# Unread identity products in TensorE's opening waits, and other owners for two PSUM tiles of the last group

## The chip, the cores and the metric

The kernel is one program on one core of a Trainium2 chip. A core has five engines that run side by side, each through its own queue of instructions in order: TensorE (PE, matrix products into PSUM; PEld is its weight load), VectorE (DVE), ScalarE (ACT), GpSimd (POOL) and SyncE (SP, which here only issues DMAs). SBUF is the working memory of 128 partitions. PSUM is the memory that TensorE writes and VectorE and ScalarE read. The metric is device time of one execution in microseconds (us).

## The reference

Two stages follow each other. The first is a delta-rule recurrence for 4 batches of 8 heads, 768 steps, 48 dimensions, in fp32:

```
k_n = k / (norm(k) + 1e-6)
for t in range(768):
    y[t]  = q[t] @ state
    state = state + beta[t] * outer(k_n[t], v[t] - k_n[t] @ state)
```

The second takes the 3072 x 384 result as x and computes a feed-forward layer of three branches with a maximum:

```
h   = max(max(x @ w1, x @ w2), x @ w3)      # 384 -> 768
out = h @ w_out                              # 768 -> 384
```

## The kernel before, in words

**Tiling.** The 768 steps are cut in 12 chunks of 64. Inside a chunk the recurrence becomes a triangular system whose inverse `ut` is made on VectorE (the generator `solve`, L507, one column per step) and applied by small matrix products. Four blocks of 32 steps and 4 batches by 8 heads fill the 128 partitions of one solve. Two chunks (512 tokens) are a group; there are six. The feed-forward layer of a group (`ffn`, L1213) runs between the pieces of the next group's recurrence.

**Order.** Everything stands under a manual schedule: each engine runs its instructions in the order in which the program emits them. The opening is a straight list of calls, from L1298 on, followed by `ffn(0)`. In it `turn` (L322) transposes keys or queries of a unit by TensorE into the PSUM tile `p_t`, which ScalarE or VectorE copies out (L344). `gram` (L404) makes the products of keys with keys, and of keys with queries, in `p_g` (L415), copied out by ScalarE at L426 and L432. `some(solving, HB + 1)` lets VectorE run the solver of the first group (L561 and L565, then a transpose at L573), and copies to `ut` follow on VectorE and ScalarE (`placed`, L505). After that come, for chunk 0, `halves_z` (`p_e`, L685), `halves_u` (`p_f`, L696), `join_z` (`p_z`, L713), `join_u` (`p_j`, L726), `new` (`p_u`, L771), `to_y` (`p_y`, L813) and `to_x` (`p_x`, L832). Each needs a copy out of PSUM of the one before it (L688, L700, L717, L728, L776, L817, L839). Between them VectorE and ScalarE unpack weights (`weights`, L230, with its work at L247 to L263), and VectorE makes transposes (L630, L632, L645, L647) and masks (L399). Then `ffn(0)` begins with `p_h` (L1224), and chunk 1 and the solver of the second group run between its products.

**A helper that exists before.** `busy(n, of)` (L1290) takes a tile `p_w` from the PSUM pool `ps_ffn` (two buffers, shared with `p_h`, `p_o` and `p_e` of L1163) and multiplies the identity by `of` n times into it; nobody reads the tile. It is called once, `busy(6, ident)`, ahead of the first transposes.

**The last group.** Its first layer is done by `crossed_hidden` (L1125) in six units of eight products, four products and a `yield`, then four more. The function `bank(n)` hands out the PSUM tile of product n: 0 to 5 from a pool of six buffers (`p_c`), 6 and 7 from the two buffers of `ps_ffn` (`p_e`). Products 0, 2, 3 and 4 are copied out by ScalarE (L1184, L1190, L1193, L1197). Products 1, 5, 6 and 7 are added by VectorE (`result`, L1169 and L1171), which in the units of odd number also adds four sums (L1198 to L1201) ahead of 5, 6 and 7. The second layer (`outputs`, L969) then takes the same two `ps_ffn` buffers as `p` and `q` for its products (L985).

Of the kernel before, what the change touches and what calls it, by code (L numbers as in the profile page):

```python
# [23 lines left out]
def kernel(  # L24
# [31 lines left out]
    nc = tc.nc  # L56
# [10 lines left out]
    TOK = 512  # L67
# [21 lines left out]
    def ps_ffn(shape, name):  # L89
        return psum.tile(shape, FP32, name=name, tag="ffn", bufs=2)  # L90
# [10 lines left out]
    ident = const.tile([128, 128], FP32, name="ident")  # L101
# [34 lines left out]
    def place(n):  # L136
        return n % NK if n < 12 else n % 4
# [82 lines left out]
    def fetch(queue=nc.scalar):  # L220
        if fetched[0] < len(pieces):
            _, src, (a, b) = pieces[fetched[0]]
            st = work.tile([128, 2 * 384], U32, name="w_bits", bufs=5)
            queue.dma_start(
                out=st.rearrange("p (a b) -> p a b", a=a), in_=src
            )
            staged.append(st)
            fetched[0] += 1
# [93 lines left out]
    def turn(n, parts=(0, 1), copy=nc.scalar.copy):  # L322

        if n not in kqts:
            if n == 6:
                kqts[n] = work.tile([128, KT, TOK], FP32, name="xt").rearrange(
                    "p k t -> p (k t)"
                )[:, 0 : NP * 4 * C].rearrange(
                    "p (j b i t) -> p j b i t", b=2, i=2, t=C
                )  # L330
            else:
                kqts[n] = work.tile([128, NP, 2, 2, C], FP32, name="kqt", bufs=6)
        kqt = kqts[n]
        p_t = ps_two("p_t")
        for i in parts:
            src = (kpad[place(n)], qpad[n % NQ])[i]
            for j in range(NP):
                nc.tensor.transpose(
                    p_t[:, i, j * 128 : (j + 1) * 128],
                    src[:, 2 * j : 2 * j + 2],  # L340
                    ident,
                )
        some = slice(parts[0], parts[-1] + 1)
        copy(  # L344
            kqt.rearrange("p j b i t -> p i (j b) t")[:, some],
            p_t.rearrange("p i (x t) -> p i x t", t=C)[:, some],
        )
# [291 lines left out]
    def halves_t(c, parts=(0, 1)):  # L639
        if c not in fine:  # L640
            fine[c] = [square("t") for g in range(2)]
        src = [ut[c % NU][:, g].rearrange("p h x -> p (h x)") for g in range(2)]
        dst = [t.rearrange("p h x -> p (h x)") for t in fine[c]]
        if 0 in parts:
            nc.vector.transpose(out=dst[0], in_=src[0])  # L645
        for bb in range(2) if 1 in parts else ():
            nc.vector.transpose(out=dst[1][rows(1 - bb)], in_=src[1][rows(bb)])  # L647
# [25 lines left out]
    def span(hs):  # L673
        return slice(hs[0], hs[-1] + 1)

    def halves_z(c):
        if c > 1:
            halves_t(c)
        at = [ats[2 * c + g] for g in range(2)]
        second = ut[c % NU].rearrange("p g h (f two x) -> p g h f two x", two=2, x=HB)  # L680
        for hs, p_v, copy in heads_of(c, "p_e", BL):
            for i, h in enumerate(hs):
                for bb, g in TILES:
                    r = rows(bb)
                    nc.tensor.matmul(  # L685
                        p_v[rows(bb ^ g), g, i], at[g][r, h], second[r, g, h, :, 1]
                    )
            copy(zs[c % NU][:, :, span(hs)], p_v)  # L688
# [436 lines left out]
    def crossed_hidden(m, hs):  # L1125

        banks = upper_pool("banks")
        xt, vec = xts[m], nc.vector.tensor_tensor  # L1130
        plus = vec if m == GROUPS - 1 else nc.gpsimd.tensor_tensor
        lo, hi = slice(0, 256), slice(256, 512)
        a11, a12, a13 = (xt[:, t, lo] for t in range(KT))
        a21, a22, a23 = (xt[:, t, hi] for t in range(KT))
        spare = [t.rearrange("p a h d -> p (a h d)") for t in kmore]
        s1, s2, s3, s4 = (spare[0][:, 256 * n : 256 * (n + 1)] for n in range(4))
        parts = [
            work.tile([128, 2, HB * BL + HB], FP32, name=name, bufs=1).rearrange(
                "p s r -> p (s r)"
            )  # L1140
            for name in ("x_bl", "y_bl")
        ]
        vec(out=s3, in0=a11, in1=a21, op=ALU.subtract)
        vec(out=s1, in0=a21, in1=a22, op=ALU.add)
        vec(out=s2, in0=s1, in1=a11, op=ALU.subtract)
        vec(out=s4, in0=a12, in1=s2, op=ALU.subtract)
        x_sums[m] = s1, s2, s3, s4
        for j in range(FT):
            hs[j] = square("h").rearrange("p h c -> p (h c)")
        for unit in range(2 * PAIRS):  # L1150
            j, i = divmod(unit, 2)
            w = {
                name: t[:, 128 * j : 128 * (j + 1)]
                for name, t in thirds[1 + i].items()
            }
            top, bottom = hs[j], hs[j + PAIRS]
            held = parts[unit % 2]
            m1, m5, m6, m7 = (held[:, 256 * n : 256 * (n + 1)] for n in range(4))
            c11 = spare[1][:, 256 * (unit // 2 % 2) :][:, 0:256]

            def times(to, *terms):
                for n, (stays, moves) in enumerate(terms):
                    nc.tensor.matmul(  # L1163
                        to, w[stays], moves, start=(n == 0), stop=(n == len(terms) - 1)
                    )

            def result(h, base, p, spare=None):
                to = h if i == 0 else base if spare is None else spare
                vec(out=to, in0=base, in1=p, op=ALU.add)  # L1169
                if i:  # L1170
                    nc.vector.scalar_tensor_tensor(  # L1171
                        out=h, in0=h, scalar=0.0, in1=to, op0=ALU.max, op1=ALU.max
                    )

            def bank(n):
                if n > 5:
                    return ps_ffn([128, TOK], "p_e")[:, 0:256]
                return banks.tile([128, TOK], FP32, name="p_c", tag="one", bufs=6)[
                    :, 0:256
                ]  # L1180

            p = bank(0)
            times(p, ("b11", a11))
            nc.scalar.copy(m1, p)  # L1184
            p = bank(1)
            times(p, ("b21", a12), ("c1", a13))
            result(top[:, lo], m1, p, c11)
            p = bank(2)
            times(p, ("t3", s3))
            nc.scalar.copy(m7, p)  # L1190
            p = bank(3)
            times(p, ("t1", s1))
            nc.scalar.copy(m5, p)  # L1193
            yield
            p = bank(4)
            times(p, ("t2", s2))
            nc.scalar.copy(m6, p)  # L1197
            plus(out=m6, in0=m6, in1=m1, op=ALU.add)  # L1198
            plus(out=m1, in0=m6, in1=m5, op=ALU.add)
            plus(out=m7, in0=m7, in1=m6, op=ALU.add)  # L1200
            plus(out=m5, in0=m5, in1=m7, op=ALU.add)  # L1201
            p = bank(5)
            times(p, ("c2", a13), ("b22", s4))
            result(bottom[:, lo], m1, p)
            p = bank(6)
            times(p, ("t4", a22), ("c1", a23))
            result(top[:, hi], m7, p)
            p = bank(7)
            times(p, ("c2", a23))
            result(bottom[:, hi], m5, p)  # L1210
            yield
# [64 lines left out]
    def some(gen, n):  # L1276
        for _ in range(n):
            if next(gen, gen) is gen:
                break
# [7 lines left out]
    nc.vector.memset(warm, 1.0)  # L1287
    nc.scalar.sqrt(warm, warm)

    def busy(n, of):  # L1290
        p_w = ps_ffn([128, TOK], "p_w")[:, 0 : of.shape[1]]
        for _ in range(n):
            nc.tensor.matmul(p_w, ident, of)

    def keys(n, queues=one_queue, copy=nc.scalar.copy):
        gram(n, (0,), queues, copy)

# [30 lines left out]
    keys(4)  # L1328
    keys(5)
    turn(6, (0,))  # L1330
    turn(0, (1,))
    load_q(3, (nc.gpsimd, nc.gpsimd))
    load_beta()
    keys(6)
    gram(0, (1,), None, later=True)
    turn(7, (0,))
    turn(1, (1,))
    keys(7)
    turn(2, (1,))
    gram(1, (1,), None, later=True)  # L1340
    turn(3, (1,))
    some(conv, 1)
    gram(2, (1,), None, later=True)
    gram(3, (1,), None, later=True)
    some(solving, HB + 1)
    halves_t(0)
    halves_z(0)
    first_norms()
# [4 lines left out]
    blocks(1, nc.gpsimd)  # L1353
    for _ in range(2):
        fetch(nc.gpsimd)
    halves_u(0)
    turn_t1(0)
    join_z(0)
    masked(pts[0], by_par(pts[0]))
# [2 lines left out]
    masked(pts[1], by_par(pts[1]))  # L1362
    old_k(0)
    old_q(0)
    new(0)
    some(conv, 1)
    fetch(nc.gpsimd)
    load_v(1, nc.gpsimd)
    placed(1, 3)
    to_y(0)  # L1370
    halves_t(1)
    solving = solve(1)
    some(solving, 1)
    to_x(0)
    some(conv, 1)


# [177 lines left out]
```

## Time and profile before

| What | Value |
|---|---|
| Median of three runs | 509.49 us (506.69, 509.49, 509.79) |
| Profiled execution, its own time | 507.8 us |
| Its span, first to last instruction | 506.1 us |
| PE busy | 484.4 us, 96% of the span |
| DVE busy | 362.5 us, 72% |
| ACT / POOL busy | 168.7 us / 186.4 us |
| Mean granted clock of TensorE | 0.969 of full speed |
| Time idle on PE from 0 to 63.3 us | 14.3 us of 63.3 us |

The span is drawn in 40 slices of 12.65 us. In the row of an engine a digit is its busy share in tenths; in the row PEclk it is the clock that TensorE was granted, in tenths of full speed. Lines with a letter L name the line of the program that issued an instruction. "Idle before" gives how long the engine stood still ahead of an instruction and what ended that. A busy TensorE is not one at full speed, so its busy share and its clock are read side by side.

### The profile page before, as it was taken

How to read it: one execution, taken by the hardware profiler on the slowest of the kernel's cores; microseconds unless marked ns; L12 is line 12 of the kernel's file. 1: busy time of each engine (PE TensorE's matmuls, PEld its weight loads, DVE VectorE, ACT ScalarE, POOL GpSimd, SP SyncE). 2: the span in 40 equal slices, each digit the busy share in tenths (PEclk: the TensorE clock that was granted, in tenths of full speed). 3: DMA queues.
4: the chain of work that ended last, by engine and by line, in shares of the span. 5: the costliest groups of instructions: out<-in, count | busy, mean ns of one | idle time of the engine just before them, and what ended most of it. 6: DMA issues, size and time to landing. Idle time of an engine off the chain costs nothing.

```text
span 506.1 us, 18677 instructions
## 1 busy us (share of the span) xinstructions
PE 484.4 (96%) x8064; PEld 338.0 (67%) x8064; DVE 362.5 (72%) x835; ACT 168.7 (33%) x320; POOL 186.4 (37%) x311
## 2 busy tenths in 40 slices
PE   7678899999999999999999999999999999999996
PEld 6567688756565555565555565555797457998795
DVE  5888989868996431799562999565998865467843
ACT  4576854884422142210153200252211042113210
POOL 6424582783491925870495870601000020000000
PEclk9855999999999999999999999999999999999999
DMA  8937979783055925443585552834224321330002
GB/s 111 205 53 207 201 177 147 183 220 91 2 141 128 191 57 122 121 118 99 120 157 124 138 139 62 168 56 93 63 61 88 62 66 25 89 80 0 0 17 47
DMA packets 109122, 53.50 MB, mean 106 GB/s; under 512 B 92209, under 2 KB 102865, under 8 KB 109041
## 3 DMA queue, kind: packets, MB, share of 16 engines
q1 hardware_dynamic: 97280, 31.78, 31.2%
q0 software_dynamic: 9216, 19.85, 15.6%
q8 instruction: 63, 1.03, 0.9%
q10 hardware_dynamic: 2544, 0.69, 0.7%
q14 instruction: 19, 0.15, 0.1%
HBM read 39.17 MB, written 13.11 MB: 103 GB/s over the span
## 4 chain that ended last, share of the span: by engine, by line
PE 82%; DVE 6%; DMA 5%; ACT 2%; issue 1%; SPq 1%; POOL 1%; ACTq 0%; DVEq 0%; POOLq 0%
PE p_h L1224 31%; PE p_o L985 13%; PE p_o L1262 12%; PE p_c L1163 4%; PE p_g L415 3%; PE p_u L771 3%; PE p_m L905 2%; PE p_k L743 2%; PE p_y L813 2%; PE p_q L743 2%; PE p_s L794 2%; PE p_j L726 2%; DMA x_bl<-at_d 1%; DMA qall<-in_q_dram 1%; PE p_e L1163 1%
## 5 line engine op out<-in xcount | busy, mean ns | idle before, releaser
L1224 PE MATMUL p_h<-xt,w_sb 128*128 128x512 f32 (+1 forms) x450 | 187.5, 559 | 1.3 <-issue 0.7
L1224 PEld LDWEIGHTS p_h<-xt,w_sb 128*128 128x128 f32 x450 | 82.5, 193 | 70.0 <-issue 62.4
L1238 DVE TENSOR_TENSOR h<-h,p_h 128x512 f32<-128x512 f32 (+1 forms) x42 | 25.4, 606 | 47.2 <-PE p_h L1224 45.7
L565 DVE TENSOR_TENSOR y_bl<-y_bl,tmp 128x31 f32<-128x31 f32 (+20 forms) x139 | 50.3, 362 | 4.8
L561 DVE TENSOR_TENSOR tmp<-x_bl,y_bl 128x31 f32<-128x31 f32 (+20 forms) x139 | 48.7, 350 | 3.9
L1262 PE MATMUL p_o<-wo_sb,h 128*128 128x384 f32 x144 | 48.9, 490 | 0.0
L373 POOL DMA_DIRECT2D turned<-in_q_dram x72 | 39.1, 551 | 4.3 <-POOL turned L368 2.9
L1262 PEld LDWEIGHTS p_o<-wo_sb,h 128*128 128x128 f32 x144 | 26.8, 190 | 17.2
L1234 ACT ACTIVATE h<-p_h 128x512 f32<-128x512 f32 x24 | 14.3, 597 | 69.3 <-PE p_h L1224 69.2
L263 POOL TENSOR_TENSOR w_sb<-mant,up 128x384 int32<-128x384 int32 x18 | 18.8, 1046 | 37.7 <-DVE mant L259 34.7
L415 PEld LDWEIGHTS p_g<-kqt 48*64 48x64 f32 x1216 | 24.9, 143 | 9.3 <-issue 6.7
L415 PE MATMUL p_g<-kqt 48*64 48x64 f32 (+1 forms) x1216 | 28.1, 243 | 0.9 <-ACT kqt L344 0.8
L1268 ACT COPY o_sb<-p_o 128x384 f32<-128x384 f32 x12 | 5.7, 479 | 62.6 <-PE p_o L1262 56.5
L399 DVE TENSOR_TENSOR pt<-p_g,mask 128x512 f32<-128x512 f32 x20 | 13.8, 689 | 16.2 <-PE p_g L415 16.0
L801 DVE TENSOR_TENSOR st<-st,p_s 48x768 f32<-48x768 f32 (+1 forms) x18 | 17.1, 949 | 11.1 <-PE p_s L794 10.8
L598 POOL DMA_DIRECT2D ut<-y_d x4 | 2.6, 651 | 60.4 <-DMA y_d<-y_bl 60.4
L148 POOL DMA_DIRECT2D v_t<-in_v_dram x14 | 11.5, 829 | 36.0 <-PE p_u L771 36.0
L368 POOL MEMSET turned<- 128x96 f32 x18 | 3.3, 191 | 49.6 <-DVE kqt L389 49.6
L771 PEld LDWEIGHTS p_u<-v_t,ut 64*64 64x64 f32 x768 | 13.7, 144 | 7.9 <-issue 5.9
L432 ACT COPY at<-p_g 128x512 f32<-128x512 f32 x22 | 12.7, 583 | 18.6 <-DVE pt L399 16.1
L373 POOL DMA_DIRECT2D turned<-in_k_dram x32 | 17.4, 553 | 1.2 <-POOL turned L368 1.2
L129 POOL DMA_DIRECT2D kpad<-in_k_dram x24 | 16.4, 691 | 3.0 <-PE p_s L794 3.0
(241 smaller groups left out, 909.2 us busy)
## 6 DMA issues: line engine op xcount, KB each, us to landing
w_bits<-in_moe_w_dram SPq DMA_DIRECT2D x9, 384.0 KB, 5.8
w_bits<-in_moe_w_dram POOLq DMA_DIRECT2D x9, 384.0 KB, 6.3
turned<-in_q_dram POOLq DMA_DIRECT2D x72, 48.0 KB, 2.8
out_dram<-o_sb SPq DMA_DIRECT2D x36, 96.0 KB, 2.3
y_x<-y SPq DMA_DIRECT2D x32, 96.0 KB, 2.2
qall<-y_x SPq DMA_DIRECT2D x32, 96.0 KB, 2.6
v_t<-in_v_dram POOLq DMA_DIRECT2D x14, 192.0 KB, 5.0
at_d<-at SPq DMA_DIRECT2D x72, 32.0 KB, 2.5
```

The costliest lines, as they stand in the source:

```text
L263: nc.gpsimd.tensor_tensor(out=dst.bitcast(I32), in0=mant_v.bitcast(I32), in1=up_v, op=ALU.add)
L373: (queue, nc.gpsimd)[i].dma_start(out=t[p0 : p0 + 32, bb, at : at + NP * 2 * D].rearrange("p (j x) -> p j x", j=NP), in_=(k, q)[i][2 * bb ...
L415: nc.tensor.matmul(p_g[rows(bb ^ (g * i)), par, c0 : c0 + C * (1 + whole)], kq[:, 0], kq if whole else kq[:, i],)
L561: nc.vector.tensor_tensor(out=t_v, in0=row.to_broadcast(t_v.shape), in1=column.to_broadcast(t_v.shape), op=ALU.mult,)
L565: nc.vector.tensor_tensor(out=rest, in0=rest, in1=t_v, op=ALU.subtract)
L743: nc.tensor.matmul(p_b[rows(bb), par, c0 : c0 + D], kqt[g][dims(par), j, bb ^ g, i], st[dims(par), bb ^ g, g, j],)
L771: nc.tensor.matmul(p_v[rows(bb ^ g), g, i], ut[c % NU][rows(bb), g, h], rhs[rows(bb), g, h],)
L985: nc.tensor.matmul(to[:, g], a[j][:, 128 * g : 128 * (g + 1)], b[j], start=(start and g == j == 0), stop=(stop and g == 1 and j == len(a) ...
L1163: nc.tensor.matmul(to, w[stays], moves, start=(n == 0), stop=(n == len(terms) - 1))
L1224: nc.tensor.matmul(p_h, w_sb[i][:, t, f * 128 : (f + 1) * 128], xt[:, t, lo : lo + w], start=(t == 0), stop=(t == KT - 1),)
L1238: nc.vector.tensor_tensor(out=h, in0=h, in1=p_h, op=ALU.max)
L1262: nc.tensor.matmul(p_o, stays, moves, start=(n == 0), stop=(n == len(terms) - 1))
```

## The change

`busy` moves up in the file, and its second argument is the identity unless one is given. Ten calls of it are put into the opening, 76 products of 128 x 128 x 128 in fp32, each of which TensorE runs as two matmul instructions with a weight load each. And in `crossed_hidden` the two buffers of `ps_ffn` go to products 3 and 4 of a unit, while 6 and 7 take theirs from the pool of six.

```
+    def busy(n, of=None):
+        of = ident if of is None else of
+        p_w = ps_ffn([128, TOK], "p_w")[:, 0 : of.shape[1]]
+        for _ in range(n):
+            nc.tensor.matmul(p_w, ident, of)
...
             def bank(n):
-                if n > 5:
+                if n in (3, 4):
                     return ps_ffn([128, TOK], "p_e")[:, 0:256]
...
     turn(6, (0,))
+    busy(5)
     turn(0, (1,))
...
     turn(7, (0,))
+    busy(13)
     turn(1, (1,))
     keys(7)
     turn(2, (1,))
     gram(1, (1,), None, later=True)
+    busy(14)
     turn(3, (1,))
     some(conv, 1)
     gram(2, (1,), None, later=True)
     gram(3, (1,), None, later=True)
     some(solving, HB + 1)
+    busy(24)
     halves_t(0)
     halves_z(0)
...
+    busy(4)
     halves_u(0)
+    busy(2)
     turn_t1(0)
     join_z(0)
...
     old_q(0)
+    busy(3)
     new(0)
+    busy(2)
...
     to_y(0)
+    busy(5)
     halves_t(1)
     solving = solve(1)
     some(solving, 1)
     to_x(0)
+    busy(4)
     some(conv, 1)
```

## The prediction

> **What bounds the kernel now.** I read the page's slices first: is TensorE busy, and at which clock?
>
> ```profile
> PE   7678899999999999999999999999999999999996
> ...
> PEclk9855999999999999999999999999999999999999
> ```
>
> From slice 7 on PE is full. Only the first five slices (63 us) have gaps, 14.3 us of them, and only there the clock falls. So both parts of the change aim where time can be found: the opening, and one wait at the end. Next the opening in stretches of 2 us (columns: PE, PEld, DVE, ACT, POOL busy, granted clock, DMA share, GB/s):
>
> ```profile
> 18.00:20.00 2.00, 0.23 (x3) 0.00 (x0) 1.63 (x9) 0.88 (x2) 2.00 (x5) 1.00 1.10 317
> 20.00:22.00 2.00, 1.66 (x37) 1.41 (x37) 1.79 (x7) 0.58 (x1) 1.60 (x3) 0.73 1.23 211
> ...
> 32.00:34.00 2.00, 2.00 (x82) 2.00 (x81) 1.50 (x5) 1.64 (x4) 0.00 (x0) 0.50 0.27 42
> ...
> 48.00:50.00 2.00, 2.00 (x121) 1.75 (x122) 1.86 (x5) 0.92 (x2) 0.00 (x0) 0.94 0.87 212
> ...
> 62.00:64.00 2.00, 2.00 (x5) 1.56 (x5) 1.90 (x6) 1.98 (x4) 0.00 (x0) 0.50 0.68 136
> ```
>
> Cut into 0.2 us, the clock changes at 20.92, 48.21, 61.88 and 65.29: twice at half speed, for 27.3 and 3.4 us. The distances are 8, 4 and 1 times 3.41 us, so the grant is decided on a grid of 3.41 us, here with borders at 31.16, 34.57, 37.98, 41.39 and 44.80. It was lost over 17.5 to 20.92, where PE idled 2.10 us, and over 58.47 to 61.88, where it idled 1.27 us and ran 32- and 48-row products. It came back over 44.80 to 48.21, which was mostly full-array `p_h`. It did not come back over 31.16 to 34.57, although PE was busy for 3.3 of 3.41 us, on 64 x 64 products. What fills the array counts, it seems, not only being busy.
>
> [...]
>
> Third, TensorE's timeline, for the waits that are to be filled:
>
> ```profile
> 17.58 0.66 PE L338 MATMUL p_t<-ident,kmore 128*128 128x128 f32 x4
> 20.34 0.63 PE L338 MATMUL p_t<-ident,qall 128*128 128x128 f32 x4 [2.10 <-DMA qall<-in_q_dram]
> ...
> 25.37 1.09 PE L338 MATMUL p_t<-ident,qall 128*128 128x128 f32 x4 [1.24 <-DMA qall<-in_q_dram]
> 26.39 1.99 PE L415 MATMUL p_g<-kqt 48*64 48x64 f32 x64
> 30.59 0.43 PE L685 MATMUL p_e<-ut,at 64*64 64x32 f32 x6 [2.21 <-ACT ut L505]
> ...
> 45.39 2.93 PE L1224 MATMUL p_h<-xt,w_sb 128*128 128x256 f32 x6 [0.57 <-ACT xt L839]
> ...
> 60.46 0.31 PE L726 MATMUL p_j<-z,t 32*32 32x32 f32 x11 [1.27 <-issue]
> 61.77 2.86 PE L1224 MATMUL p_h<-xt,w_sb 128*128 128x256 f32 x6
> ```
>
> **Price of one added product.** `p_w` has only run cold: 12 instructions for 6 products in 2.9 us, 0.235 us each, 0.47 a product. Warm I bound it by `p_h` of 256 columns, six in 1.30 us, half of 0.217 for half the columns (0.108 an instruction), and by `p_x` of 128 columns at 73.3, six in 0.68 us (0.113). I take 0.113, the row of the same width: 0.226 a product. All 76 cost 17.2 us warm, 36 us cold. Nothing reads `p_w`, it waits for nothing but PE itself, and no other engine has work in those PSUM buffers here; what is queued behind is PE's own next real product.
>
> **The opening, block by block, warm.** The 5 (1.1 us) stand in the wait of 0.85 us before 15.54 and push it by 0.2; the 2.10 us wait behind takes that. The 13 (2.9) go from 18.05 to 21.0, where q's transpose began at 20.34: 0.7 late. But the clock now has no gap in which to fall at 20.92; `p_t`, `p_g`, `p_t`, `p_g`, which took 3.8 us cold, take 2.0, and are done at 23.0 instead of 24.1. The 14 (3.2) then end at 26.15, past the 25.24 at which the DMA frees the transpose: its copy on ScalarE comes 0.25 us later, and so do the unpacking, the two `pt` copies and the `ut` copies queued behind (29.49 and 30.54 before). `p_g` twice takes 1.1 instead of 2.0, to 27.7. The 24 (5.4) end at **33.1**. `ut` was complete at 31.2, so here the products overrun their wait by 1.65 to 1.9 us, and `p_e` is late by as much: it ends at 34.15 where it ended at 33.05.
>
> Behind it the pieces shorten: a cold `p_e`, `p_f`, `p_z`, `p_j`, `p_u`, `p_y`, `p_x` took 2.2, 2.1, 1.2, 1.8, 2.1, 1.9, 1.5 us; the same groups warm (chunk 1, 48 to 74 us) 1.06, 1.06, 0.69, 0.87, 1.39, 1.08, 0.68. But between any two stands a copy, and those are no faster. I followed the queues: `p_f` to 36.05 after its 4; ScalarE's six `ut` copies to 37.3 (35.85 before); `p_z` to 37.7, `p_j` to 39.35, VectorE's `p_j` copy done 40.7 (39.62 before), its `u` copy 41.96 (41.37), its `y` copy **43.5** (43.16). The delay of VectorE melts from 1.1 to 0.3. `p_x` runs from 44.0, ScalarE's `xt` copies end at 45.35 as before, the last 4 end at 45.6, and the first `p_h` takes 1.45 instead of 2.93: it ends at 47.05, not 48.32. **TensorE leads by 1.25 us, VectorE trails by 0.3.**
>
> That lead is not yet a gain. From 45.4 to 58.5 VectorE is hardly idle (0.31 us at 50.4, which takes the 0.3): second solver, masks, transposes. `p_j` of chunk 1 starts at 58.58 on VectorE's transpose of L632, and that comes when it came. So at 58.5 the opening nets 0, with bounds of -1.5 (overruns halved) and +1.9 (the overrun at `p_e` kept).
>
> Behind 58.5 the lead may count. PE waited 1.27 us in the middle of `p_j` for nothing that the profile shows; with 304 instructions more ahead and PE standing 1.8 us before `p_j`, that stall need not be met at this place. Each gives about the same: without the stall 1.27; with the clock kept, `p_h` at 61.85 takes 1.49 instead of 2.79, 1.30. I count one of them, **-1.3**, with ends of 0 and -2.6. From 65 us on PE is full, so what is won by then reaches the end.
>
> **The last group.** Both queues at the hand-over, ScalarE's line first, then VectorE's, then PE's:
>
> ```profile
> 476.79 0.37 ACT L1197 COPY y_bl<-p_c 128x256 f32<-128x256 f32 x1
> ```
> ```profile
> 479.58 0.41 DVE L1169 TENSOR_TENSOR y_bl<-y_bl,p_e 128x256 f32<-128x256 f32 x1
> ```
> ```profile
> 477.89 1.03 PE L1163 MATMUL p_e<-xt,w_sb 128*128 128x256 f32 x4
> 480.05 1.24 PE L985 MATMUL p_o<-wo_sb,h 128*128 128x192 f32 x6 [1.14 <-DVE y_bl L1169]
> ```
>
> The first `p_o` needs the buffer of product 6, which VectorE gives back at 480.0. With products 3 and 4 as owners ScalarE gives both back by 477.2. Its operand, `h` of the early results, is there from 476.4. So PE goes on at 478.9: **-1.14**. What is late next: the sums for the third product (VectorE, 481.17 to 482.2), needed at 484.85 then, so nothing. Inside the stage each buffer is used once per unit of 4.75 us as before, and the longest holder, product 7 of an odd unit, lets go 1.4 us ahead of the next unit's product 6. No loss there. End 0 only if another wait hides in these 1.14.
>
> **Sum.** 0 - 1.3 - 1.14 = -2.4 us against the profiled 507.8: 505.4. The median stands 1.7 above that execution, so the forecast is **507.0 us**.
>
> **Rivals.**
> - *All warm and nothing overrun.* If the products are shorter, or waits longer, than I hold them, `p_e` starts at 31.2 warm, VectorE's `y` copy comes 1.2 us earlier and both terms behind 58.5 fall due: -1.2 - 2.6 - 1.14 = -5, so 504.5. For: idle time plus what halved pieces free is about 9 + 9 = 18 us, near the 17.2 added. Against: three blocks exceed their own wait by the rows.
> - *The overrun is kept; slower.* The place is `p_e`, 1.9 us late; the point is whether the clock holds at the border of 41.39. From 37.98 to there PE would run `p_j`, 3 products and `p_u`, mostly small tiles, as in the window that lost the clock at 61.88. If it falls, `p_y` (1.9 for 1.08) and 7 products at double price put the `y` copy some 0.8 us further back, and VectorE carries 1.9 + 0.8 to 58.5: +2.7 - 1.14 = +1.6, so 511.1. It decides once VectorE's delay at its `y` copy is over 1.5 us (1.14 and 0.3). If the clock also falls under the 24 before `p_e` (0.47 each until a border of the grid), 2 to 4 us more, 513 to 515.
> - *The products don't do what they say.* The clock falls all the same in the small tiles and the opening ends even: only -1.14, 508.3.
>
> [...]
>
> **Numbers.** Forecast 0.45 (with its bounds 505.0 to 509.0), all warm 0.22, overrun kept 0.18, only the end 0.15. The range of 8 in 10 takes in both outer cases without their tails: 503.0 to 511.4. Within 1% (5.1 us, about what a measurement here can tell from no change) lie 504.4 to 514.6: faster 0.22, since half of the all-warm case and a tail of the forecast reach below, same 0.70, slower 0.08, the cold overrun.
>
> **What would show it.** Right: granted clock 1.00 through 20 to 48; `p_e` of chunk 0 at about 33, waiting for nothing; first `p_h` near 45.6 in 1.45 us; no wait at the first `p_o` of the last group. Wrong: a clock of 0.5 between 38 and 45, a product at over 0.25 us, `p_e` still waiting for ScalarE (then the products are cheaper than I priced them), or VectorE's L632 before 58.5 moved by over 1 us from its old place.

## The result, and the profile after

| | Before | Changed |
|---|---|---|
| Median of six runs | 509.12 us (506.69 to 510.99) | 514.35 us (513.24 to 516.63) |
| Ratio to before, 95% interval | | 1.0103 (1.0075 to 1.0132) |
| Span of the profiled execution | 506.1 us | 511.5 us |
| Mean granted clock of TensorE | 0.969 | 0.998 |
| PE busy / instructions | 484.4 us / 8064 | 493.4 us / 8216 |

The change costs 5 us. The forecast was 507.0 with a range to 511.4, so sign and range are wrong. In the profiled execution its first aim is reached in full all the same. The same two rows of the page as in the prediction, now of the changed kernel:

```profile
PE   7898799999999999999999999999999999999996
...
PEclk9999999999999999999999999999999999999999
```

In this execution the clock is never withheld between 7 and 509 us, and still the span is 5.5 us longer. This execution is the shortest of the six; the five others had a mean clock of 0.989 to 0.992 instead of 0.998, by an estimate from these means some 6 to 9 us more at half speed. The chain that ended last, of the changed kernel, in order of time (start, us, what), tells where the products stand:

```profile
13.44 5.94 DMA kmore<-in_k_dram
19.38 0.14 issue
19.52 0.63 PE p_t L338 x4
20.15 2.90 PE p_w L681 x26
...
25.32 3.32 PE p_w L681 x28
...
30.45 5.55 PE p_w L681 x48
36.01 1.06 PE p_e L692 x64
37.07 1.09 PE p_w L681 x8
```

The 13, 14 and 24 products, 11.8 us of them, lie on the chain in full, with nothing but real work between them, and this stretch of it starts with the keys' DMA that lands at 19.38. `p_e` of chunk 0 starts at 35.94 instead of 30.59. Now TensorE's timeline behind it, and the place where the lost time of before stood (`p_j`, 1.27 us):

```profile
50.63 1.46 PE L1231 MATMUL p_h<-xt,w_sb 128*128 128x256 f32 x6
...
55.49 0.44 PE L801 MATMUL p_s<-u,kpad 64*64 64x48 f32 x14 [1.52 <-issue]
...
60.51 0.56 PE L750 MATMUL p_k<-st,kqt 48*64 48x48 f32 x21 [1.33 <-issue]
...
66.44 0.50 PE L733 MATMUL p_j<-z,t 32*32 32x32 f32 x35 [0.27 <-issue]
66.88 1.15 PE L750 MATMUL p_q<-st,kqt 48*64 48x48 f32 x64
67.95 1.56 PE L1231 MATMUL p_h<-xt,w_sb 128*128 128x256 f32 x6
```

The first `p_h` is warm (1.46 us for 2.93), and so is the one that ran cold at 61.77. But TensorE stops for 1.52 and 1.33 us in the middle of `p_s` and `p_k`, for nothing that the profile names; there were 0.69 us (in `p_h`, at 55.37) and 1.27 us (in `p_j`) of that before. At the hand-over of the last group the wait of 1.14 us is gone:

```profile
484.75 1.03 PE L1170 MATMUL p_c<-xt,w_sb 128*128 128x256 f32 x4
485.62 1.14 PE L992 MATMUL p_o<-wo_sb,h 128*128 128x192 f32 x6
```

The same instructions side by side give the lag of the changed kernel: +4.0 us at the end of `p_e`, +4.2 at VectorE's `y` copy, +3.8 at the end of the first `p_h`, +7.2 at VectorE's `v_t` (L762) behind the two stalls, +4.9 at chunk 1's `p_u` (the warm `p_h` gave back 1.4), +6.9 at the start of the last group, +5.5 at its end.

### The profile page after: what moved, and what is told of

Its sections match the earlier page's. It is cut to its first block, busy times and chain, and to the rows that moved or that the text cites. A ratio compares the mean times of both kernels' runs of the same rounds, so it can differ in the third digit from the quotient of the medians.

```text
span 511.5 us, 18981 instructions
## 1 busy us (share of the span) xinstructions
PE 493.4 (96%) x8216; PEld 347.4 (68%) x8216; DVE 361.8 (71%) x835; ACT 169.3 (33%) x320; POOL 187.5 (37%) x311
## 3 DMA queue, kind: packets, MB, share of 16 engines
q0 software_dynamic: 9216, 19.85, 16.4%
## 4 chain that ended last, share of the span: by engine, by line
PE 81%; DVE 7%; DMA 6%; issue 2%; SPq 1%; POOL 1%; ACT 1%; DVEq 0%; POOLq 0%
PE p_h L1231 28%; PE p_o L992 12%; PE p_o L1269 12%; PE p_c L1170 5%; PE p_g L415 3%; PE p_w L681 3%; PE p_m L912 2%; DMA kmore<-in_k_dram 2%; PE p_u L778 2%; PE p_y L820 2%; PE p_k L750 2%; DMA qall<-in_q_dram 2%; PE p_s L801 2%; SPq L129 1%; PE p_q L750 1%
## 5 line engine op out<-in xcount | busy, mean ns | idle before, releaser
L1231 PE MATMUL p_h<-xt,w_sb 128*128 128x512 f32 (+1 forms) x450 | 184.7, 552 | 0.2 <-issue 0.2
L1231 PEld LDWEIGHTS p_h<-xt,w_sb 128*128 128x128 f32 x450 | 80.9, 190 | 68.2 <-issue 62.1
L561 DVE TENSOR_TENSOR tmp<-x_bl,y_bl 128x31 f32<-128x31 f32 (+20 forms) x139 | 51.2, 369 | 3.9
L565 DVE TENSOR_TENSOR y_bl<-y_bl,tmp 128x31 f32<-128x31 f32 (+20 forms) x139 | 48.5, 349 | 4.8
L1269 PEld LDWEIGHTS p_o<-wo_sb,h 128*128 128x128 f32 x144 | 26.7, 190 | 17.2
L415 PEld LDWEIGHTS p_g<-kqt 48*64 48x64 f32 x1216 | 23.3, 134 | 9.3 <-issue 6.4
L415 PE MATMUL p_g<-kqt 48*64 48x64 f32 (+1 forms) x1216 | 26.5, 233 | 1.0 <-ACT kqt L344 0.8
L681 PE MATMUL p_w<-ident 128*128 128x128 f32 x164 | 22.2, 291 | 3.0 <-POOL ident masks.py:199 2.0
L681 PEld LDWEIGHTS p_w<-ident 128*128 128x128 f32 x164 | 20.4, 202 | 3.5 <-POOL ident masks.py:199 2.0
```

What stands on the lines that cost most here:

```text
L415: nc.tensor.matmul(p_g[rows(bb ^ (g * i)), par, c0 : c0 + C * (1 + whole)], kq[:, 0], kq if whole else kq[:, i],)
L561: nc.vector.tensor_tensor(out=t_v, in0=row.to_broadcast(t_v.shape), in1=column.to_broadcast(t_v.shape), op=ALU.mult,)
L565: nc.vector.tensor_tensor(out=rest, in0=rest, in1=t_v, op=ALU.subtract)
L1231: nc.tensor.matmul(p_h, w_sb[i][:, t, f * 128 : (f + 1) * 128], xt[:, t, lo : lo + w], start=(t == 0), stop=(t == KT - 1),)
L1269: nc.tensor.matmul(p_o, stays, moves, start=(n == 0), stop=(n == len(terms) - 1))
```

## The experiments

Theory A: products that outlast their waits delay the real ones. Theory B: the added instructions themselves cost, at the points where TensorE stops for nothing that the profile names. Theory C: the keys' DMA landed late by chance in the one profiled run. All ratios are to the kernel before on the same chip, and the lists give the counts of the ten blocks in the order of the program (changed kernel: 5, 13, 14, 24, 4, 2, 3, 2, 5, 4).

### The parts

Edit of `e1_banks_only`: all ten calls removed, the two PSUM tiles kept.

```
-    busy(5)   ... and the nine other calls
```

> Only the change of the two PSUM tiles, none of the ten product blocks. All theories of the opening agree: the opening is that of before (clock at half speed from about 21 to 48 us), the first p_o of the last group starts with no wait, and the time falls by the 1.14 us of that wait: about 508.0 us, ratio to before 0.998.

Measured: 0.9928 (0.9897 to 0.9958). The wait at the first `p_o` is gone as expected, but the gain is larger than its 1.14 us (0.22%). The opening of this kernel is a test of theory C too. TensorE's timeline of this kernel, with no product in the way:

```profile
18.99 1.11 PE L338 MATMUL p_t<-ident,kmore 128*128 128x128 f32 x4
20.09 1.08 PE L338 MATMUL p_t<-ident,qall 128*128 128x128 f32 x4
...
30.65 0.43 PE L692 MATMUL p_e<-ut,at 64*64 64x32 f32 x6 [2.20 <-ACT ut L505]
```

The keys' transpose came at 18.99 instead of 17.58, and it did no harm: the wait for the queries behind it, 2.10 us in the trace of before, is simply not there. In all 18 profiles that transpose starts between 17.2 and 19.9 us, in the five without any of the ten blocks between 17.2 and 19.0, so most of that is scatter, not the change's doing. Theory C is right as far as the late landing goes; that it costs anything is due to the products behind it.

Edits of the three others: `e2_no24` has 0 for the 24; `e3_early_only` has 5, 13, 14, 24 and no late ones; `e4_late_only` has only the six late ones.

```
e2_no24:         busy(5)  busy(13)  busy(14)  -          and the six late ones
e3_early_only:   busy(5)  busy(13)  busy(14)  busy(24)   and none of the late ones
e4_late_only:    -        -         -         -          and the six late ones
```

> The changed kernel without the block of 24. Theory A (blocks longer than their waits delay the real products): p_e of chunk 0 starts as soon as ut is complete, some 2 us earlier than 35.94, and the time falls by 2 to 3 us to 511.5 to 512.3. Theory B (the cost is the 304 added instructions, each 256th of which stalls TensorE while its instructions are fetched): only 96 of 304 instructions go, 1 us or less is won, 513.4 or more. Theory C (the keys' DMA landed 1.9 us late by chance in the one profiled run): turn 7 starts at 17.6 here, and at 19.5 again by A with a cause.

> The changed kernel with the first four blocks (5, 13, 14, 24) and without the six late ones (20 products). A: the late blocks stand on the chain for most of their 4.95 us; if the clock holds without them the time falls by 3 to 4 us to 510.5 to 511.5; if the clock falls at a border between 38 and 45 us, 2 to 3 of these are lost again, 513. B: 80 fewer instructions, 513.5 or more.

> The changed kernel without the first four blocks, with the six late ones. A: p_e of chunk 0 starts at 31.2 again, but cold, and the 20 products at 0.47 us each cost 9.4 us less about 2 us of waits until the clock comes back; with one border crossed on the way about +3 to +5 in the opening less 1.1 at the end: 511 to 513.5. B: 80 instructions instead of 304, about a quarter of the loss: 509.5.

Measured: `e2_no24` 1.0061 (1.0016 to 1.0106), `e3_early_only` 1.0059 (1.0031 to 1.0087), `e4_late_only` 1.0117 (1.0046 to 1.0187). Removing either half gives back some 0.4%, which the intervals hardly tell from nothing. Without the 24, `p_e` ends at 34.24 instead of 37.07, but the clock falls at 30.70 and the late products run cold; the first `p_h` ends at 52.51, no earlier than with the 24 (52.09). With the late ones alone it is the same: `p_e` ends at 32.88 as in before, the `y` copy 3.5 us later than in before. Without the late ones the clock falls at 41.70 and the first `p_h` is cold, yet the `y` copy ends at 48.21, only 0.85 us behind the changed kernel's 47.36. Theory A fits these places, but `e4_late_only`, with 80 added instructions, also shows seven stalls of 0.35 to 1.77 us "for nothing", 7.7 us in all.

### Instructions without time, time without instructions, blocks that fit

Edit of `e5_tiny` and `e6_wide`:

```
e5_tiny:  each product   p_w[0:32, 0:32] = ident[0:32, 0:32] @ ident[0:32, 0:32]
e6_wide:  5, 13, 14, 24 of 128 columns  ->  1, 3, 4, 6 of 512 columns of kpad[0]
```

> The changed kernel with every added product cut to 32 x 32 x 32: the same 304 instructions at the same places, hardly any array time (about 20 ns an instruction by p_z, 3 us in all, most of it in waits), and no full-array work that would hold the clock. Theory A (array time longer than the waits): as with the two PSUM tiles alone, 507.4, plus 0 to 1 us; the clock falls near 21 as before. Theory B (304 more instructions, a fetch stall at each 256th): about as slow as the changed kernel, 512 or more, with stalls at 1985, 2241, 2497.

> The changed kernel with its first four blocks made of products of 512 columns (1, 3, 4 and 6 of them, keys as the moving operand, 12.2 us instead of 12.7) and a quarter of the instructions (56 instead of 224). Theory A: as slow as the changed kernel, 513 to 514. Theory B: 168 of 304 added instructions are gone, 2 to 3 us faster, 511 to 512.

Edit of `e7_fitted` and `e8_fitted_early`, the counts of the ten blocks:

```
-    5, 13, 14, 24,  4, 2, 3, 2, 5, 4
+    3,  3,  9, 16,  0, 1, 0, 0, 2, 1      # e7_fitted
+    3,  3,  9, 16,  0, 0, 0, 0, 0, 0      # e8_fitted_early
```

> The changed kernel with blocks cut to what the waits hold at the warm price of 0.226 us: 3, 3, 9, 16 early, then none before p_f, 1 before p_z, none, none, 2 before p_x, 1 before p_h. Theory A: p_e of chunk 0 starts at 31.2 again, warm, and ends 1 us earlier than in before; the time is that of the two PSUM tiles alone, 507.4, or up to 2 us less. If products cost more than the waits hide even so, 508.5 to 511. Theory B: 140 instructions, 509.5.

> Only the four early blocks of that fitted version (3, 3, 9, 16). Theory A: p_e warm at 31.2; the clock falls between 38 and 42 and p_h runs cold; within 1 us of the two PSUM tiles alone, 506.5 to 508.5. Beside the fitted version it tells what a warm p_h at 45 us is worth: by the traces so far nothing, since VectorE is the bound until 58 us.

Measured: `e5_tiny` 1.0050 (1.0020 to 1.0080), `e6_wide` 1.0163 (1.0107 to 1.0219), `e7_fitted` 1.0104 (1.0063 to 1.0146), `e8_fitted_early` 1.0072 (1.0038 to 1.0106).

`e5_tiny` is not the clean test it was meant to be: small products on one corner of the array took 0.06 us an instruction at half clock (48 in 2.76 us), not 0.02, and delayed the first `p_h` by 2.7 us against `e1_banks_only`. `e6_wide` has 136 added instructions instead of 304 and is the slowest of all, by only three executions, against theory B as I had put it (the number of instructions). Its profiled execution took 531.7 us at a mean clock of 0.941, the three others 515.6 to 519.5 us at 0.982 to 0.989, so its trace is left out of the table of times below.

`e7_fitted` is the run that broke theory A as the whole answer. Its opening came near what was hoped, although the clock fell from 38.05 to 44.88: `p_e` ended at 33.83 and VectorE's `y` copy at 44.02, 0.8 and 0.9 us behind before, and the first `p_h` ran warm and ended at 47.62, 0.7 us ahead of before. Then, in TensorE's and VectorE's timelines of this kernel:

```profile
53.78 0.24 PE L703 MATMUL p_f<-z,t 64*64 64x32 f32 x2 [1.60 <-issue]
...
60.83 0.91 PE L750 MATMUL p_q<-st,kqt 48*64 48x48 f32 x47
65.89 0.76 PE L750 MATMUL p_q<-st,kqt 48*64 48x48 f32 x17 [4.15 <-issue]
```
```profile
69.62 0.42 DVE L1245 TENSOR_TENSOR h<-h,p_h 128x256 f32<-128x256 f32 x1 [4.08 <-PE p_h L1231]
```

A product group of 64 is cut in two, TensorE stands for 4.15 us, and VectorE stands for 4.08 us behind it. When all that the trace shows of TensorE (weight loads, products and some 130 waits for semaphores) is numbered from 0 in order of start, this stall lies before number 2753, the one at 53.78 before 2241; in the changed kernel they lie before 1985, 2241, 2497 and 2753; in before, 2241 and 2497. **In every trace the stalls of this kind of over 0.4 us lie 256 instructions apart, or a multiple of it**, up to number 12225; the only exceptions are two gaps of 0.43 us, one each in `e7_fitted` and `e8_fitted_early`. I call these places borders. The queue table of the changed kernel's page (packets, MB, share of the DMA engines) has one row that fits pieces of that kind:

```profile
q8 instruction: 64, 1.05, 0.9%
```

64 packets of 16.4 kB each, and TensorE's 16566 numbers make 64.7 blocks of 256; in before there are 63 packets, and 16259 numbers make 63.5 blocks. By these counts I take the packets of q8 for TensorE's. In the changed kernel's trace those that start between 47 and 57 us took 1.1 to 2.3 us.

The traces hold these packets one by one, and they show what a stall goes with. Count the packets from 1 and set packet n beside the border at number 193 + 256 n. In all 18 traces no border is passed less than 1.2 us after its packet has landed (1.29 us at the least in before, 1.26 in the changed kernel), and after a stall of over 0.1 us TensorE goes on 1.2 to 1.8 us behind that landing, whether it stood for 0.1 us or for 4.15. In the changed kernel the packet for border 2497 started 1.23 us after TensorE had passed the border before, took 2.27 us, and TensorE went on 1.52 us later: 5.02 us from border to border, of which 1.33 were idle. For the 4.15 us of `e7_fitted` the three terms are 4.56, 1.44 and 1.48 us. My estimate from these terms is that a border stalls when TensorE needs less time for its 256 instructions than the three take together. Two groups of 64 small products with their weight loads are 256 instructions, and they take 2.1 us where the clock is full (1.06 us for the 64 of `p_e` at 36.01 in the changed kernel). After some stalls the clock fell too: in before it went to half for 3.41 us at 61.88, 1.42 us after the end of the 1.27 us in `p_j`, and in four others (`e4_late_only`, `e8_fitted_early`, `e12_wide256`, `e14_products_only`) for 3.4 us within 1.5 us of the end of one of 1.2 to 1.8 us. In the changed kernel it stayed full after 1.52 and 1.33 us, so that the stall brought the fall about is not shown.

Most borders cost nothing here, but nine of the changed kernel's cost 0.1 to 1.5 us each, and one of `e7_fitted` 4.15 us.

### Moving the borders

Edit of `e9_pad12` and `e13_pad6`: the two PSUM tiles alone, plus 12 or 6 tiny products in a wait of 0.84 us at 12 us.

```
     some(solving, 1)
+    tiny(12)          # e13_pad6: tiny(6)
     keys(4)
```

> The two PSUM tiles alone, plus 12 unread products of 32 x 32 x 32 in the 0.84 us wait before p_g at 12.92: 48 instructions and some 0.3 us beyond the wait, which the later waits absorb. 48 is what 304 leaves over 256, so from there on the fetch borders (each 256th instruction of TensorE) fall on the same work as in the changed kernel. Theory B (where the borders fall sets the stalls): stalls of 4 to 5 us in all instead of 2, 509.5 to 511 instead of 507.4. Theory A (only array time counts): 507.4 to 507.8.

> The same with 6 such products, 24 instructions, a third position of the borders. Theory B: another sum of stalls, anywhere from 2 to 8 us, and the time moves with it: 507 to 513. Theory A: 507.4.

Measured: `e9_pad12` 1.0049 (1.0012 to 1.0085), `e13_pad6` 1.0021 (0.9993 to 1.0049), against 0.9928 and 0.9967 without a pad (the second further below; these two were measured on other chips, each against the kernel before there). The pad itself is hidden: `p_e` of chunk 0 starts at 29.90 with 12, earlier than in before. But a border now falls into the last product of `p_y`, which VectorE's `y` copy waits for, and another into `p_u` at 116 us. From two stretches of `e9_pad12`'s TensorE timeline:

```profile
43.31 0.34 PE L825 MATMUL p_y<-u,pt 64*64 64x48 f32 x1 [1.34 <-issue]
...
116.56 0.43 PE L783 MATMUL p_u<-v_t,ut 64*64 64x48 f32 x12 [1.63 <-issue]
```

Forty-eight instructions that cost no time of their own cost 0.8 to 1.2%. That is theory B in a second form: what counts would be where the borders fall, not how many instructions there are.

Edit of `e10_aligned64` and `e12_wide256`, both with 256 added instructions, so that the borders fall on the same work as with none:

```
e10_aligned64:   24 products of 128 columns  ->  12 of 128 columns
e12_wide256:     24 products of 128 columns  ->  12 of 256 columns of kpad[0]
```

> The changed kernel with 12 products instead of 24 before p_e: 64 products, 256 instructions, so that the borders fall on the same work as with no products. Theory A: p_e some 2 us earlier, 512 to 512.5. A and B together: the stalls also fall back to about 2 us, 509 to 510.

> The changed kernel with the 24 products before p_e replaced by 12 of 256 columns (keys as the moving operand): the same 5.2 to 5.5 us of array time in half the instructions, 256 added ones in all, borders as with no products. Theory A: 513 to 514.5, as the changed kernel. B: stalls of 2 us instead of 5, 511 to 512.

Measured: `e10_aligned64` 0.9994 (0.9968 to 1.0019), `e12_wide256` 1.0035 (1.0003 to 1.0067). The borders are back: the group of `p_j` is again cut before its last 11 products, as in before. TensorE's timeline, `e10_aligned64` first:

```profile
62.51 0.31 PE L733 MATMUL p_j<-z,t 32*32 32x32 f32 x11 [0.90 <-issue]
```
```profile
63.21 0.31 PE L736 MATMUL p_j<-z,t 32*32 32x32 f32 x11 [1.73 <-issue]
```

The stalls are not as short as I expected, though: 4.4 and 3.6 us in all, not 2. Twelve products fewer before `p_e` let it end at 32.86; `e12_wide256` keeps the overrun (35.63).

### The parts on one chip

Edits of `e14_products_only` and `e15_mix280`, against the changed kernel (`wide` has 256 columns of kpad[0] as its moving operand); `e16_changed_again` and `e17_banks_again` are the changed kernel and `e1_banks_only` unaltered.

```
-                if n in (3, 4):           # e14_products_only
+                if n > 5:
...
-    busy(24)                              # e15_mix280: 280 added instructions
+    wide(6); busy(12)
```

> The ten blocks of products, the two PSUM tiles as before the change. If the tiles are worth just the wait at the first p_o, 1.1 us more than the changed kernel on the same chip (0.2%); if they are worth what their first comparison gave, 3.7 us more (0.7%). The wait of 1.14 us stands again before the first p_o.

> The changed kernel with its block of 24 made of 6 products of 256 columns and 12 of 128: the same array time, 280 added instructions, borders 24 away from those with none (the changed kernel is 48 away). If the number of instructions counts, between the version with 256 (ratio 1.0035) and the changed kernel with 304 (1.0103), 1.007. If only the place of the borders counts, as the pads of 24 and 48 instructions moved the kernel with the tiles alone (0.9928 to 1.0021 and 1.0049), 1.009 to 1.013.

> The changed kernel on the chip of the other three, to compare with them. Ratio to before 1.0103 again, 1.0075 to 1.0132; stalls at the 256th instructions at p_u near 119 us and p_z and p_j near 185 us again.

> The two PSUM tiles alone once more, on the chip of the other three. The wait at the first p_o alone gives a ratio of 0.998; the first comparison gave 0.9928 (0.9897 to 0.9958). If it is 0.998 here, the rest of the first was scatter between runs.

Measured: `e14_products_only` 1.0125 (1.0094 to 1.0157), `e15_mix280` 1.0084 (1.0052 to 1.0116), `e16_changed_again` 1.0078 (1.0048 to 1.0108), `e17_banks_again` 0.9967 (0.9938 to 0.9996). On one chip the products cost 1.1% (1.0078 against 0.9967), 5.7 us. The tiles bring 0.3% without them and 0.5% with them; the wait of 1.14 us (0.22%), which stands in the trace of `e14_products_only` again, lies within the intervals of both comparisons; only that of `e1_banks_only` (0.9897 to 0.9958) lies wholly beyond it. The line of `e14_products_only`, from its TensorE timeline cut off at 490 us:

```profile
489.34 0.92 PE L992 MATMUL p_o<-wo_sb,h 128*128 128x192 f32 x4 [1.14 <-DVE y_bl L1176]
```

`e15_mix280` equals the changed kernel, which tells neither form of theory B from the other. In `e16_changed_again` the longer stalls stand at places where the changed kernel has them too, with other lengths, here from its TensorE timeline:

```profile
54.95 0.44 PE L801 MATMUL p_s<-u,kpad 64*64 64x48 f32 x14 [1.34 <-issue]
...
59.42 0.56 PE L750 MATMUL p_k<-st,kqt 48*64 48x48 f32 x21 [0.78 <-issue]
```

### All profiles side by side

Times are those of the profiled execution of each; "stalls" adds TensorE's gaps of over 0.05 us at the 256-instruction borders.

| Kernel | Added instr. | Ratio | `p_e` ends | `y` copy ends | between | first `p_h` ends | Stalls |
|---|---|---|---|---|---|---|---|
| before | 0 | 1 | 33.05 | 43.16 | 10.11 | 48.32 | 2.1 |
| e1_banks_only | 0 | 0.9928 | 33.11 | 43.20 | 10.09 | 48.37 | 2.0 |
| e17_banks_again | 0 | 0.9967 | 33.27 | 43.37 | 10.10 | 48.54 | 1.3 |
| e13_pad6 | 24 | 1.0021 | 33.53 | 43.64 | 10.11 | 48.81 | 4.4 |
| e9_pad12 | 48 | 1.0049 | 32.35 | 44.24 | 11.89 | 49.41 | 4.8 |
| e4_late_only | 80 | 1.0117 | 32.88 | 46.70 | 13.82 | 50.25 | 7.8 |
| e8_fitted_early | 124 | 1.0072 | 33.63 | 43.84 | 10.21 | 49.00 | 7.4 |
| e7_fitted | 140 | 1.0104 | 33.83 | 44.02 | 10.19 | 47.62 | 8.8 |
| e2_no24 | 208 | 1.0061 | 34.24 | 48.96 | 14.72 | 52.51 | 3.1 |
| e3_early_only | 224 | 1.0059 | 37.17 | 48.21 | 11.04 | 53.37 | 2.7 |
| e10_aligned64 | 256 | 0.9994 | 32.86 | 45.61 | 12.75 | 49.16 | 4.4 |
| e12_wide256 | 256 | 1.0035 | 35.63 | 45.48 | 9.85 | 49.03 | 3.6 |
| e15_mix280 | 280 | 1.0084 | 37.98 | 50.64 | 12.66 | 54.18 | 4.2 |
| e5_tiny | 304 | 1.0050 | 34.95 | 45.89 | 10.94 | 51.05 | 4.4 |
| e14_products_only | 304 | 1.0125 | 38.02 | 48.21 | 10.19 | 52.39 | 5.9 |
| changed | 304 | 1.0103 | 37.07 | 47.36 | 10.29 | 52.09 | 5.2 |
| e16_changed_again | 304 | 1.0078 | 36.48 | 47.83 | 11.35 | 51.74 | 3.6 |

In these single profiles the sum of the stalls follows what the added instructions leave over multiples of 256, and not their number. It is 4.2 to 4.4 us for 24 and 280, 3.6 to 5.9 for 48 and 304, and largest, 7.4 to 8.8, from 80 to 140; with 208 and 224 it is down to 3.1 and 2.7. (`e6_wide`, with 136, has 7.9.) Only the two with 256 depart from this: they do not fall back to the 1.3 to 2.1 us of none. `e8_fitted_early` shows what stalls cost almost without an overrun: its first `p_h` ends only 0.5 to 0.6 us later than in the two profiles with the tiles alone, its stalls are 5.4 to 6.1 us longer, and its ratio is 1.0072 against 0.9967 and 0.9928, which is 5.3 and 7.3 us.

## Why the prediction was wrong, step by step

**Price of a product: right.** 0.226 us was taken; 26 instructions took 2.90, 28 took 3.32, 48 took 5.55, so 0.223 to 0.237.

**The clock: right for the profiled run**, where it is full from 7.3 to 509.1 us. In before the stretches at one clock between 7.27 and 505.61 us last 13.65, 27.31, 13.65, 3.41 and 440.32 us, which are 4, 8, 4, 1 and 129 times 3.413. In three other profiles with all ten blocks it fell for one or two windows of 3.4 us between 37.9 and 49.6 us (`e10_aligned64`, `e15_mix280`, `e16_changed_again`), about the place that the second rival named, and by their mean clock it fell in the other five executions of the changed kernel too, at places that no trace shows.

**`p_e` at 33.1: mis-sized, 35.94.** The step "the 2.10 us wait behind takes that" took the order in which two DMAs landed in one execution for a property of the program. Of the 2.84 us between, 1.94 is the keys' transpose at 19.52; the rest is small differences in the blocks and the pieces between them. In a program without products the late keys eat the wait for the queries (`e1_banks_only`); the 13 products need it behind them, and so keys, 13, 14 and 24 add up. The overrun is 4.0 us at the end of `p_e`, not 1.1. Halving the 24 took `p_e` back to its old place and, with the borders moved as well, the ratio to 0.9994 (`e10_aligned64`).

**"The delay of VectorE melts from 1.1 to 0.3": failed.** Between the end of `p_e` and the end of the `y` copy lie 10.1 us in before at half clock and 10.3 in the changed kernel at full clock. Most of it is VectorE's queue from its copy of `p_e` to its last mask ahead of the `u` copy, in before and then in the changed kernel:

```profile
33.19 0.42 DVE L688 COPY z<-p_e 128x256 f32<-128x256 f32 x1 [0.44 <-PE p_e L685]
...
39.65 0.69 DVE L399 TENSOR_TENSOR pt<-pt,mask 128x512 f32<-128x512 f32 x1
```
```profile
37.14 0.42 DVE L695 COPY z<-p_e 128x256 f32<-128x256 f32 x1 [1.72 <-PE p_e L692]
...
43.62 0.69 DVE L399 TENSOR_TENSOR pt<-pt,mask 128x512 f32<-128x512 f32 x1
```

That is 7.16 and 7.18 us, and 7.1 to 7.2 in 16 of the 18 traces: the faster `p_f`, `p_z` and `p_j` gave nothing there, since each waits for a copy, a transpose or an unpacking that is queued on ScalarE or VectorE. I had listed these queues and still let the shorter products through. In the 2.8 to 3.0 us behind it VectorE does wait for TensorE (`p_u`, `p_y`), and there the chain of the changed kernel holds 1.5 us of late products. Over the whole stretch TensorE is idle for 0.9 us in before and 0.7 in the changed kernel: the late products took what the clock had freed. No run keeps the clock full through the stretch without them, so what it is worth there alone stays unmeasured. Where the clock falls while late products stand there, the stretch grows to 12.7 (`e10_aligned64`). The 4.0 us went to the `y` copy whole.

**The lead of TensorE: right in kind, without worth, as said.** The first `p_h` gains 1.47 us; with its start 5.2 us late there was no lead.

**"-1.3, the stall need not be met at this place": failed, with the sign.** I took 1.27 us "for nothing that the profile shows" for an accident. It is one of a row at every 256th instruction, and 304 more instructions put the row elsewhere. In the two profiles of the changed kernel it costs 5.2 and 3.6 us in all, in before 2.1. The pads of 24 and 48 instructions show that such a shift alone costs 0.5 to 1.2%; the sum of the stalls is 2.7 us or more in every kernel of the table with added instructions and 2.1 or less in those without. The cold `p_h` did go (1.3), as I had offered as the other half.

**The last group, -1.14: right** in the trace (`p_o` waits for nothing), and of the right size within the intervals of two of three comparisons. Whether the tiles bring more than that wait stays open.

**The sum, put right.** Spans of single executions don't add up to 1%: the two profiles with the tiles alone, the same kernel, are 3.7 us apart (503.5 and 507.2 us), and the changed kernel's span is 8.1 us over the one and 4.3 over the other. Over both profiles of each kernel, the first `p_h` ends 3.5 us later with the products, and the stalls behind it are 2.1 us longer. Together that is 5.5 us, near the 5.7 that the times on one chip give; with two profiles each, the nearness is in part luck.

**The rivals.** "The overrun is kept" named the right place and the right sign, and its point was met (VectorE 4.2 us late at the `y` copy, over 1.5). But its price rests on a fallen clock, and in the profiled execution the delay came without one; 511.1 was too low, for it knew nothing of the keys' scatter and of the borders. The 8% for slower by over 1% were too few: all the bounds came from one execution's waits, and every error in them counts on the same side, because a wait that is shorter than its filler costs and one that is longer gives nothing.

**Open.** What delays a packet of instructions: two profiles of the changed kernel show stalls of 1.01 and 0.19 us at the same border, 1.33 and 0.78 at another, and among the long ones the packet starts 0.7 to 5.7 us after TensorE has passed the border before; no trace shows why. So executions of one kernel differ, and the sizes at one place are no constants: `e10_aligned64`, with the borders back in their old places, had 4.4 us of stalls, in `p_h`, `p_j`, `p_u` and `p_g`, where before and the two profiles with the tiles alone have theirs too, but fewer in each. And how the 1.1% of the products divides exactly between overrun and borders: `e10_aligned64` and `e12_wide256` have the same borders and differ by 2.8 us at the end of `p_e`, but in their profiles the clock fell in that stretch in the first and not in the second, and they come out even at the `y` copy.

The best kernel of the study is the two PSUM tiles alone, 0.9928 and 0.9967 of before.

## What to carry to other kernels

A wait can be filled only if it is there in every execution and ends behind the filler: here the wait of 2.10 us for the queries' DMA stood in the trace of before and was not there in that of `e1_banks_only`, where the keys' transpose ahead of it came at 18.99 instead of 17.58 us, and the 13 products that the changed kernel has between the two stood on its chain for 2.90 us. A faster clock brought nothing in a stretch that TensorE did not bound for the most part and in which fillers took back what it freed (10.1 us from `p_e` to the `y` copy at half clock, 10.3 at full clock with them); compare the time from copy to copy at both clocks before paying for it. And instructions that cost no time of their own still moved the borders behind them (ratios of 1.0021 and 1.0049 with pads of 24 and 48, 0.9928 and 0.9967 without), so a change of a few dozen instructions to an engine that runs many small ones is to be judged against a pad of the same length, not against the old kernel.

## What the runs showed of the hardware that I had not expected

In these traces TensorE's stalls of over 0.4 us "for nothing" lie 256 instructions apart or a multiple of it, with the two exceptions of 0.43 us, and it passed no such border less than 1.2 us after the packet set beside it had landed (1.29 us in before, 1.26 in the changed kernel). The changed kernel's two longest stalls, 1.52 and 1.33 us, stand in a stretch with small products and many DMAs (53 to 61 us: 211 matmul instructions, 199 GB/s against a mean of 105); the longest of all is 4.15 us (`e7_fitted`), most are of 0.3 to 1.8, and the profile puts them down as idle "issue", mostly in the middle of a group. Unread products of 32 x 32 in one corner of the array took 0.04 us an instruction at full clock (24 in 0.94 us in `e9_pad12`), a third of one of 128 x 128 (0.112 to 0.119 in the changed kernel's chain), though they have a sixteenth of its array and a quarter of its columns. And being busy did not bring the clock back by itself: in `e5_tiny` TensorE was busy with small products for all of a window of 3.41 us (32.29 to 35.70) and stayed at half clock (the 64 instructions of `p_f` from 35.44 took 1.93 us, 1.14 at full clock in the changed kernel). In before the clock came back at the end of two windows, which held 2.85 us (44.80 to 48.21) and 2.75 us (61.88 to 65.29) of 128 x 128 products; the least in a window of the 17 traces at whose end it came back is 1.2 us. In `e8_fitted_early` it did not come back over 44.08 to 47.50, with 2.85 us of them.
